# Which free slot a load takes, and when it may take the last one: a decode attention kernel with one slab of 31 slots

## The chip, the cores and the metric

The kernel runs on one core of a Trainium2 chip. The metric is the time of one execution on the device, in microseconds (us). Times of the profile are counted from the start of its span, which is the first instruction of the profiled execution.

## What is computed

Two layer kinds alternate, each is applied twice, and both passes of attention read the same caches.

```python
Bn, D = 8, 448                  # one new token for each of 8 sequences
Hq, Hkv, Sk, Dh = 16, 8, 4096, 256
def A(x):                       # attention over cached K and V, no mask
    q = x @ wq                  # (8, 16, 1, 256)
    p = softmax(q @ k_cache.T / 16)      # each K head serves two q heads
    return (p @ v_cache) @ wo
def B(x):                       # h shifted along a sequence of length 1, so the first
    ...                         # w1/w2 part adds nothing; what is left:
    return x + gelu(layernorm(x) @ w3) @ w4
x = x + A(layernorm(x));  x = x + B(layernorm(x))
x = x + A(layernorm(x));  x = x + B(layernorm(x))
```

K and V are 8 sequences x 8 heads x 4096 x 256 in bf16, 134 MB each. They don't fit on the chip, so most of them is read twice, and 447 MB come from HBM in one execution.

## The kernel before

**Units and steps.** A unit is `(pass, sequence b, head g)`: the scores, the softmax and the product with V of one K/V head. Pass 1 is the first attention layer and pass 2 the second. The list `units` holds 128 units and some empty places (`GAP`) in a written-out order: for each sequence b the heads of pass 1, then a layer end where the dense layers of that sequence run (spread over steps by the generator `mid_steps`), then pass 2. To have work for the gap, two heads of other sequences (`loose`, `ahead`, `lone`) are drawn into it. A unit takes four steps, and step number i is 4 x (place of the unit) + quarter. In step i the main loop calls `transposes(i)`, then `k_part` (16 products with one transposed quarter of K), on the first steps of a unit the softmax of the unit before it (`max_mms`, `exps`, `to_rows`, `sums`), then `v_part` for the quarters of V that `plan` puts there, some six steps after their K, and one piece of the dense layers.

**Slots.** All of K and V passes through one SBUF tile, `slab`, cut into 31 slots of 512 KB (128 partitions x 2048 bf16). A slot holds a quarter of a unit's K as loaded (raw), a quarter of its K transposed (`kt`), or a quarter of its V. The list `free` says which slots the program may fill. `transposes` takes a free slot for the transposed quarter, lets VectorE (DVE) transpose into it with two instructions at L562, and puts the raw slot on the list; `v_part` (products at L630) and `k_part` (L653) put their slot on the list once its products are issued. In pass 1 the transposed K of heads 2 to 7 (`KEEP`) isn't given back: it stays in the slab for pass 2 of the same sequence, apart from two quarters that are parked in PSUM (copied back by ScalarE at L520).

**Loads.** The order of all loads is fixed beforehand in `loads`. `pump`, called after every slot that comes free, issues from that list on the SP queue (L536) as long as more than `RESERVE` = 1 slot is free, so one slot is always left for the next transposition. A load is a quarter (512 KB, a single) or two neighbouring quarters into slots x and x + 1 with x even (1 MB, a pair), where the list allows it (`wide`). Where it is also in `firm`, and at least seven quarters are under way, the load waits for two neighbouring slots rather than go out as a single. SP runs its queue in order: a load whose slot is still being read holds up all loads behind it.

`take` gives the lowest number among the free slots whose neighbour isn't free, or else the lowest of all; `take_two` gives the lowest free even pair. The list `free` itself is in the order in which the program gave the slots back.

**Who waits.** DVE does the transpositions and, in the same queue, the two maxima (L668, L686) and the sum (L727) of the softmax; PE needs the first maximum for its products at L676. Two transpositions of a quarter are due in step i for K that is used in step i + 1 (`LEAD`) and beyond; `by[i]` says how many quarters must be transposed by then, evenly over a stretch between layer ends, so most are transposed 5 to 18 steps ahead of use. `transposes` returns early where the next quarter isn't yet due and either its load hasn't been issued or no slot is free.

Of the kernel before, what the change touches and what calls it, by code (L numbers as in the profile page):

```python
# [15 lines left out]
UNIT = 2048  # L16
N_SLOTS = 31
RESERVE = 1
KEEP = 6
PARKED = 2  # L20
RUN = 2
# [10 lines left out]
def kernel(  # L32
# [164 lines left out]
    def flush():  # L197
        while between:
            between.pop(0)()
# [162 lines left out]

    heads = list(range(G))
    loose = heads[: G - KEEP]

# [5 lines left out]
    lone = {b: [(1, b + 2, g) for g in loose] for b in range(4)}  # L373
# [24 lines left out]
    def fresh(u, s):  # L398

        return u is not GAP and (u[0] == 1 or u[2] in loose)  # L400
# [4 lines left out]
    t = 0  # L405
# [21 lines left out]
    parts = [(t, s) for t in range(n_units) for s in range(4) if fresh(units[t], s)]  # L427
# [16 lines left out]
    for t in order:  # L444
        for s in range(4):
            i = late_v.get((t, s), 4 * t + s + LAG)
            if t in ends or units[t + 1 : t + 2] == [GAP]:
                i = 4 * t + (6, 6, 7, 7)[s]
            elif t + 2 == n_units:
                i = 4 * t + (7, 8, 8, 8)[s]  # L450
            elif t + 1 == n_units:
                i = 4 * t + (5, 5, 6, 6)[s]
# [3 lines left out]
    loads = []  # L456
# [5 lines left out]
    for i in range(4 * n_units + 8):  # L462
# [9 lines left out]
        t, q = divmod(i + 2, 4)  # L472
# [3 lines left out]
    free = list(range(N_SLOTS))  # L476
# [3 lines left out]
    def take():  # L480

        lone = [x for x in free if x ^ 1 not in free]
        x = min(lone or free)
        free.remove(x)
        return x

    def take_two():

        both = [x for x in free if x % 2 == 0 and x + 1 in free]
        if both:  # L490
            free.remove(both[0])
            free.remove(both[0] + 1)
        return both[:1]
# [13 lines left out]
    extra.append((w4_sb[:], B_w4.rearrange("(c p) d -> p c d", p=128)))  # L507
    n_loads = [0]

    def pump():  # L510
        while loads and len(free) > RESERVE:
            kind, t, i = loads[-1]
            _, b, g = units[t]
            if kind == "p":
                loads.pop()
                x = take()
                dst = slots[x].rearrange("p (e q c x) -> p q c e x", e=4, q=2, c=4)
                for j in range(2):
                    src = park[parked[g, i]][j][:].bitcast(BF16)
                    nc.scalar.copy(dst[:, j], src.rearrange("p (c e x) -> p c e x", c=4, e=4))  # L520
                kt_of[(1, b, g), i] = x
                continue
            cache, of = (A_k_cache, raw_of) if kind == "k" else (A_v_cache, v_of)
            n, two = 1, (kind, t, i + 1)
            if i % 2 == 0 and two in wide and two in loads[-PAIR_VIEW:]:
                x = take_two() if len(free) > RESERVE + 1 else []
                if x:
                    n, x = 2, x[0]
                    loads.remove(two)
                elif under_way[0] >= ENOUGH and two in firm:  # L530
                    return
            loads.pop()
            if n == 1:
                x = take()
            src = cache[b, g].rearrange("(p s e) d -> p s (e d)", s=4, e=8)
            nc.sync.dma_start(  # L536
                slab[:, UNIT * x : UNIT * (x + n)].rearrange("p (s d) -> p s d", s=n),
                src[:, i : i + n],
            )
            for m in range(n):  # L540
                of[t, i + m] = x + m
            under_way[0] += n
            n_loads[0] += n
            if n_loads[0] >= 8 and extra:
                nc.sync.dma_start(*extra.pop(0))

    todo = list(reversed(parts))

    def transposes(i):


        while len(parts) - len(todo) < by[i]:
            t, s = todo[-1]
            if 4 * t + s > i and ((t, s) not in raw_of or not free):
                return
            todo.pop()
            raw = raw_of.pop((t, s))
            kt = kt_of[units[t], s] = take()
            src = slots[raw].bitcast(FP32).rearrange("p (q c e i) -> p q c e i", q=2, c=4, e=4)
            dst = slots[kt].bitcast(FP32).rearrange("p (e q c r) -> p q c e r", e=4, q=2, c=4)  # L560
            for q in range(2):
                nc.vector.transpose(dst[:, q], src[:, q])  # L562
            _, b, g = units[t]
            if (g, s) in parked:
                for q in range(2):
                    dst = park[parked[g, s]][q][:].rearrange("p (c e r) -> p c e r", c=4, e=4)
                    nc.vector.transpose(dst, src[:, q])
            free.append(raw)
            under_way[0] -= 1
            pump()  # L570
# [5 lines left out]
    def dense_next():  # L576
        flush()
        if dense and next(dense[0], "end") == "end":
            dense.pop(0)
# [3 lines left out]
    def make_blocks(t):  # L583

        if t in runs and t not in ready:
            p, b, g = units[t]
            if p == 1 or (b, g % 4 // 2) in q_done:
                x, n = runs[t]
                qT = qT1[:, :, b] if p == 1 else qT2[:, :, b % 2]
                expand(Qblk[x], qT[:, 4 * g : 4 * (g + n)], n, scb[t % 2])  # L590
                ready.add(t)
# [50 lines left out]
    def k_part(t, s):  # L642
        u = units[t]
        p, b, g = u
        if s == 0:
            assert t not in runs or t in ready
            scs[t] = scb[t % 2][:, 0:64].rearrange("p (c b h) -> p c b h", b=4, h=2)
        key = (u if fresh(u, s) else (1, b, g)), s
        ktv = slots[kt_of[key]].rearrange("p (e c m x) -> p e c m x", e=4, c=2, x=2)
        for c in range(2):  # L650
            for db in range(4):
                for x in range(2):
                    nc.tensor.matmul(  # L653
                        scs[t][:, 2 * s + c, :, :],
                        ktv[:, db, c, :, x],
                        Qblk[run_of[t][0]][:, run_of[t][1], db, x, :, :],
                        start=(db == 0 and x == 0),
                        stop=(db == 3 and x == 1),
                    )
        if p == 2 or g in loose or (g, s) in parked:  # L660
            free.append(kt_of.pop(key))
            pump()
# [9 lines left out]
    def max_mms(t):  # L672

        mzs[t] = scb[t % 2][:, 64:384]
        for h in range(2):
            nc.tensor.matmul(  # L676
                mzs[t][:, 128 * h : 128 * h + 128],
                pm[:, h : h + 1].to_broadcast([128, 128]),
                ident,
                start=True,  # L680
                stop=True,
            )
# [42 lines left out]
    def sums(t):  # L725
        zz = mzs[t][:, 256:320].rearrange("p (c h) -> p h c", h=2)
        nc.vector.tensor_reduce(zs, zz, AX.X, ALU.add)  # L727
        rz_of[t] = rzs[nth[t] % 2]
        if (t, 0) in late_v:
            rz_of[t] = rz_far[:, held.index(t) % AHEAD, :]  # L730
        nc.gpsimd.tensor_tensor(out=rz_of[t], in0=zs, in1=mone, op=ALU.pow)  # L731
# [60 lines left out]
    for t in range(n_units + 1):  # L792
        cur = t < n_units
        for q in range(4):
            i = 4 * t + q
            if cur:
                if t in fence and q == 0:
                    flush()
                    while (fence[t], 1) not in q_done:
                        next(dense[0])  # L800
                        flush()
                    flush()
                    make_blocks(t)
                late = q == 0 and t and not beside[t]
                if beside[t]:
                    transposes(i)
                flush()
                if not late and not beside[t]:
                    transposes(i)
                if units[t]:  # L810
                    k_part(t, q)
            back = t and units[t - 1]
            if q == 0 and back:
                max_mms(t - 1)
                exps(t - 1)
            if cur and late:
                transposes(i)
            if back and q == 1:
                to_rows(t - 1)
                sums(t - 1)  # L820
            if q == 1 and not cur:
                mark(t - 2)
            for u, s in plan.get(i, []):
                v_part(u, s)
                if s == 3:
                    head_out(u)
            if q == 3 and cur and t > 1 and t - 2 not in ends:
                mark(t - 2)
            if q == 3 and t - 1 in ends:
                mark(t - 1)  # L830
            dense_next()
            if q > 1:
                make_blocks(t + 1)
            if cur and units[t] and q == 3:
                max_reduce(t)
# [112 lines left out]
```

## Time and profile before

| | |
|---|---|
| median of 3 runs | 1114.25 us (1113.67 to 1115.25) |
| profiled execution, its own time | 1115.99 us |
| its span | 1114.2 us |
| granted TensorE clock | 1.0 |
| busy: PE, DVE, ACT, POOL | 62%, 49%, 27%, 9% |
| read from HBM | 446.77 MB |
| loads of V: 1 MB, 512 KB | 130, 252 |
| loads of K: 1 MB, 512 KB | 97, 126 |
| median time from issue to landing, V: 1 MB, 512 KB | 13.1 us, 8.1 us |
| median time from issue to landing, K: 1 MB, 512 KB | 14.0 us, 8.8 us |

In the page's second part the span is cut into 40 slices; a digit is the busy share in tenths, and the last row is what the DMA engines moved. A row of an answer about waits reads: engine, line and what it wrote, what it waited for, us in total, times, longest. A row of windows reads: the window, its length, then for each engine its busy us and number of instructions, then the granted clock, the DMA engines' mean share and GB/s. A row of the timeline reads: start, us, engine, line, operation, written <- read, number of instructions merged into the row, and in brackets the idle time of the engine before it with what ended it. Consecutive instructions of one kind are merged into one row.

### The profile page before, as it was taken

The page shows a single profiled execution, that of the slowest core. Times are in us where ns is not written, and L with a number is a line of the kernel's source. Part 1 is how long each engine was busy: PE and PEld are TensorE (multiplying, and loading weights), DVE is VectorE, ACT ScalarE, POOL GpSimd, SP SyncE. Part 2 cuts the span into 40 slices and gives each one's busy share as a digit, 9 for nine tenths or more (in the row PEclk, how much of TensorE's full clock was granted, in tenths as well). Part 3 has the DMA queues.
Part 4 walks back from the last instruction along what each step waited for, and adds up shares of the span by engine and source line. Part 5 has one row for each costly group of instructions (what it writes and reads, how often), then busy time and mean ns, then how long its engine had stood idle before and what let it go on. Part 6 is the DMA issues. An engine that isn't in the chain of part 4 may idle for free.

```text
span 1114.2 us, 46349 instructions
## 1 busy us (share of the span) xinstructions
PE 687.9 (62%) x20737; PEld 640.8 (58%) x20737; DVE 550.7 (49%) x1305; ACT 306.0 (27%) x1360; POOL 104.1 (9%) x156
## 2 busy tenths in 40 slices
PE   3345675666756576565756667565756667665766
PEld 2334565565646565565655556565656566555765
DVE  4347554654446445554455535563446535554322
ACT  1112124321233212422243212422143212422242
POOL 0001001110011100110011000110011000100011
DMA  9999999999999999999999999999999999999993
GB/s 367 394 418 425 408 417 422 424 417 395 417 423 424 400 403 419 423 424 391 414 420 424 402 410 404 420 424 415 383 421 424 409 412 404 422 423 400 371 405 128
DMA packets 94503, 449.77 MB, mean 404 GB/s; under 512 B 9936, under 2 KB 15968, under 8 KB 64864
## 3 DMA queue, kind: packets, MB, share of 16 engines
q1 hardware_dynamic: 94304, 446.81, 98.4%
q8 instruction: 162, 2.65, 0.9%
q14 instruction: 37, 0.30, 0.1%
HBM read 446.77 MB, written 0.01 MB: 401 GB/s over the span
## 4 chain that ended last, share of the span: by engine, by line
DMA 39%; PE 15%; issue 6%; ACT 6%; DVE 5%; POOL 0%; SPq 0%; DVEq 0%; ACTq 0%; POOLq 0%
DMA slab<-in_A_v_cache_dram 31%; DMA slab<-in_A_k_cache_dram 9%; PE bank L630 5%; PE bank L653 4%; DVE slab L562 3%; ACT pt L720 2%; PE bank L137 1%; ACT slab L520 1%; ACT pe L689 1%; DVE small L686 1%; PE bank L676 1%; PE bank L712 1%; ACT pt_far L720 1%; PE bank L702 1%; PE bank L313 1%
## 5 line engine op out<-in xcount | busy, mean ns | idle before, releaser
L562 DVE STREAM_TRANSPOSE slab<-slab 128x512 f32<-128x512 f32 x640 | 414.6, 687 | 214.7 <-DMA slab<-in_A_k_cache_dram 167.2
L630 PEld LDWEIGHTS <-slab 128*128 128x128 bf16 x8192 | 273.1, 106 | 286.5 <-DMA slab<-in_A_v_cache_dram 223.0
L630 PE MATMUL bank<-pt,slab 128*128 128x2 bf16 x7168 | 260.5, 166 | 232.7 <-DMA slab<-in_A_v_cache_dram 161.5
L653 PE MATMUL bank<-Qblk,slab 128*128 128x8 bf16 x8192 | 297.2, 168 | 77.4 <-DVE slab L562 39.1
L653 PEld LDWEIGHTS <-slab 128*128 128x128 bf16 x8192 | 267.8, 105 | 88.2 <-DVE slab L562 46.6
L689 ACT ACTIVATE pe<-bank,small 128x32 bf16<-128x32 f32 x256 | 61.3, 295 | 406.7 <-DVE small L686 406.7
L731 POOL TENSOR_TENSOR small<-small 128x2 f32<-128x2 f32 x112 | 78.2, 698 | 773.2 <-DVE small L727 773.2
L720 ACT CAST pt<-bank 32x64 bf16<-32x64 f32 x448 | 90.8, 203 | 106.4 <-PE bank L712 102.5
L686 DVE TENSOR_REDUCE small<-bank 128x2 f32<-128x256 f32 x128 | 54.1, 423 | 103.2 <-PE bank L676 102.9
L727 DVE TENSOR_REDUCE small<-bank 128x2 f32<-128x64 f32 x128 | 27.1, 212 | 118.5 <-ACT pt L720 102.9
L166 ACT CAST Qblk<-bank 32x32 bf16<-32x32 f32 (+1 forms) x272 | 48.2, 177 | 110.7 <-PE bank L160 108.2
L676 PE MATMUL bank<-rows,small 128*128 128x128 bf16 x256 | 48.5, 293 | 11.5 <-DVE small L668 11.5
L668 DVE TENSOR_REDUCE small<-bank 128x2 bf16<-128x64 f32 x128 | 26.4, 206 | 58.5 <-PE bank L653 58.3
L630 PE MATMUL bank<-pt_far,slab 128*128 128x2 bf16 x1024 | 37.0, 166 | 26.1 <-DMA slab<-in_A_v_cache_dram 24.4
L712 PE MATMUL bank<-pe,rows 128*128 128x64 bf16 x512 | 51.3, 241 | 1.9 <-issue 1.9
L712 PEld LDWEIGHTS <-rows 128*128 128x128 bf16 x512 | 33.8, 124 | 28.4 <-issue 28.1
L702 PE MATMUL bank<-pe,small 128*128 128x64 bf16 x128 | 27.3, 213 | 30.7 <-ACT pe L689 29.4
L182 PEld LDWEIGHTS <-wo_sb 128*128 128x128 bf16 x1152 | 35.5, 104 | 8.8 <-issue 7.7
L182 PE MATMUL bank<-OT,wo_sb 128*128 128x1 bf16 x1024 | 33.2, 165 | 5.6 <-ACT OT L599 4.5
L137 PEld LDWEIGHTS <-wq_sb 128*128 128x128 bf16 x864 | 30.6, 106 | 10.3 <-issue 5.9
L520 ACT COPY slab<-park 128x1024 bf16<-128x1024 bf16 x32 | 30.1, 1029 | 9.4 <-DVE slab L562 9.3
L599 ACT ACTIVATE OT<-bank,small 128x2 bf16<-128x2 f32 x122 | 25.4, 261 | 24.1 <-PE bank L630 22.7
(113 smaller groups left out, 386.5 us busy)
## 6 DMA issues: line engine op xcount, KB each, us to landing
slab<-in_A_v_cache_dram SPq DMA_DIRECT2D x130, 1024.0 KB, 13.1
slab<-in_A_v_cache_dram SPq DMA_DIRECT2D x252, 512.0 KB, 8.1
slab<-in_A_k_cache_dram SPq DMA_DIRECT2D x97, 1024.0 KB, 14.0
slab<-in_A_k_cache_dram SPq DMA_DIRECT2D x126, 512.0 KB, 8.8
wo_sb<-in_A_wo_dram SPq DMA_DIRECT2D x4, 896.0 KB, 11.7
wq_sb<-in_A_wq_dram SPq DMA_DIRECT2D x3, 1024.0 KB, 6.8
w_sb<-in_B_w_dram SPq DMA_DIRECT2D x1, 1568.0 KB, 12.5
w_sb<-in_B_w_dram SPq DMA_DIRECT2D x3, 448.0 KB, 16.7
```

What stands on the lines that cost most here:

```text
L137: nc.tensor.matmul(pv[:, i, j, :], cols(big[:, c, :], m + i * half), rows[:, c, :], start=(i == 0 and j == 0 and c == 0), stop=True, skip_ ...
L166: nc.scalar.copy(dst, src)
L182: nc.tensor.matmul(y[:, c, :], chunk(wo_sb[:, k, :], c), o[:, k, :], start=False, stop=True, skip_group_check=True,)
L562: nc.vector.transpose(dst[:, q], src[:, q])
L630: nc.tensor.matmul(pos[t][:, k, :], vv[:, c, 128 * k : 128 * k + 128], pts[t][:, 8 * s + c, :], start=(t == 0 and s == 0 and c == 0 and k ...
L653: nc.tensor.matmul(scs[t][:, 2 * s + c, :, :], ktv[:, db, c, :, x], Qblk[run_of[t][0]][:, run_of[t][1], db, x, :, :], start=(db == 0 and x ...
L676: nc.tensor.matmul(mzs[t][:, 128 * h : 128 * h + 128], pm[:, h : h + 1].to_broadcast([128, 128]), ident, start=True, stop=True,)
L686: nc.vector.tensor_reduce(nm, mx, AX.X, ALU.max, negate=True)
L689: nc.scalar.activation(pe[:].rearrange("p c b h -> p h (c b)")[:, h], scs[t].rearrange("p c b h -> p h (c b)")[:, h], ACT.Exp, bias=nm[:, ...
L712: nc.tensor.matmul(pp[:, c], sel, pe[:], start=True, stop=True)
L720: nc.scalar.copy(pts[t][sl].rearrange("p (k c) h -> p k c h", c=4), pp[sl, :, :, pb, :].rearrange("p c k h -> p k c h"),)
L731: nc.gpsimd.tensor_tensor(out=rz_of[t], in0=zs, in1=mone, op=ALU.pow)
```

## The change

Three things change in the schedule that is made when the program is built; no operation is added or taken out.

- `take` gives the slot that has been on the list longest, again first among those whose neighbour isn't free; `take_two` gives the pair whose younger half has been free longest.
- `spare()` takes the place of `RESERVE`: one slot is kept only where the next K to be transposed is used within `SOON` = 4 steps of the current step (`now`), else none.
- `todo`, the K quarters still to be transposed, is made before `pump`, which now reads it.

```diff
+SOON = 4
...
+    now = [0]
...
     def take():
 
         lone = [x for x in free if x ^ 1 not in free]
-        x = min(lone or free)
+        x = (lone or free)[0]
         free.remove(x)
         return x
 
     def take_two():
 
         both = [x for x in free if x % 2 == 0 and x + 1 in free]
+        both.sort(key=lambda x: max(free.index(x), free.index(x + 1)))
         if both:
...
+    todo = list(reversed(parts))
+
+    def spare():
+
+        return RESERVE if todo and 4 * todo[-1][0] + todo[-1][1] <= now[0] + SOON else 0
+
     def pump():
-        while loads and len(free) > RESERVE:
+        while loads and len(free) > spare():
...
             if i % 2 == 0 and two in wide and two in loads[-PAIR_VIEW:]:
-                x = take_two() if len(free) > RESERVE + 1 else []
+                x = take_two() if len(free) > spare() + 1 else []
...
-    todo = list(reversed(parts))
...
-            i = 4 * t + q
+            i = now[0] = 4 * t + q
```

## The prediction

> **What bounds the kernel now.** I read the page first, then windows, then the waits of the SP queue, then the timeline.
>
> ```profile
> DMA  9999999999999999999999999999999999999993
> GB/s 367 394 418 425 408 417 422 424 417 395 417 423 424 400 403 419 423 424 391 414 420 424 402 410 404 420 424 415 383 421 424 409 412 404 422 423 400 371 405 128
> HBM read 446.77 MB, written 0.01 MB: 401 GB/s over the span
> DMA 39%; PE 15%; issue 6%; ACT 6%; DVE 5%; POOL 0%; SPq 0%; DVEq 0%; ACTq 0%; POOLq 0%
> ```
>
> The DMA engines are the bound: busy in every slice but the last, while PE is busy 62% and DVE 49% of the span. Nothing removes bytes here, so time can only come from slices that move less than the best. Windows of 14 us show how much less (last two columns: DMA share, GB/s):
>
> ```profile
> 250.00:264.00 14.00, 8.15 (x234) 7.60 (x230) 4.53 (x15) 2.87 (x15) 0.70 (x1) 1.00 1.00 375
> 280.00:294.00 14.00, 9.86 (x321) 9.59 (x318) 6.50 (x13) 3.91 (x19) 1.25 (x2) 1.00 1.03 416
> 336.00:350.00 14.00, 9.54 (x299) 8.94 (x299) 9.80 (x21) 4.43 (x22) 2.09 (x3) 1.00 1.01 423
> 1036.00:1050.00 14.00, 11.23 (x359) 10.92 (x358) 4.68 (x17) 3.41 (x16) 1.24 (x2) 1.00 0.97 364
> 1050.00:1064.00 14.00, 9.57 (x295) 9.13 (x293) 4.75 (x12) 7.34 (x23) 1.40 (x2) 1.00 0.97 349
> ```
>
> Pairs (1 MB) move 423 to 425, a full run of singles (512 KB) 416. Around each layer end it falls to 350 to 400. Cutting the span into windows of 14 us and summing 14 x (1 - rate/416) over those below 416, start and tail apart, gives 18 us lost, all near the layer ends, and 1036:1064 alone 4.0. That is the most this change can win. Why it falls there:
>
> ```profile
> SPq L536 <- PE bank L630: 202.2, 174, 5.0
> SPq L536 <- DMA slab<-in_A_v_cache_dram: 138.1, 120, 5.2
> SPq L536 <- DVE slab L562: 97.6, 49, 6.0
> SPq L536 <- PE bank L653: 81.2, 64, 8.3
> ```
>
> Loads wait on SP for the release of their slot: by a V quarter's products (L630), a transposition (L562) or a K quarter's products (L653). At a layer end six heads' transposed K lie in the slab, some nine slots circulate, and each load goes out within 0.1 us of the release of a slot just freed. Adding up the trace's issues less its packets, in steps of 2 us, with the shortfall beside it: with 1 to 1.5 MiB issued and not yet moved, 8.4% of the rate is lost (62 us of the span); with 1.5 to 2, 4.1% (168 us); with 2 to 2.5, 1.5% (198 us); with 2.5 to 3, 0.4%; above, under 1%. So the price of a slot less in the air is known.
>
> **Part 1: oldest slot instead of lowest number.** No instruction is added; 832 quarters of 512 KB are loaded as before. I followed the slot lists of both programs and gave each load, as its earliest moment, the time at which the trace of before shows the last release of its slot. Example, the first dip: the third K quarter of unit 29 waits in before for a transposition
>
> ```profile
> 250.57 0.33 SPq L536 DMA_DIRECT2D slab<-in_A_k_cache_dram  x1
> 249.24 1.30 DVE L562 STREAM_TRANSPOSE slab<-slab 128x512 f32<-128x512 f32 x2
> 258.38 1.30 DVE L562 STREAM_TRANSPOSE slab<-slab 128x512 f32<-128x512 f32 x2 [4.08 <-DMA slab<-in_A_k_cache_dram]
> ```
>
> (SP's load starts as the first two transpositions end, 250.5). In the new order it takes a slot released at 249.2, 1.4 us sooner; and it is this quarter's landing for which DVE idles 4.08 us before 258.38. Of the 21 loads from 252.4 to 277.8, 12 gain 0.4 to 3.4 us, seven wait for the same release as before (six of them transpositions: 259.7, 265.9, 268.6 and so on), and two lose under 0.8. In the stretches that lose, the mean lead is 0.15 to 0.45 MiB; I take 0.25.
>
> That is half a bin above, so each bin goes half way to the next: 62 x (8.4-4.1)%/2 = 1.3, 168 x (4.1-1.5)%/2 = 2.2, 198 x (1.5-0.4)%/2 = 1.1, together 4.6 us. Against it: what moves sooner is no longer outstanding, so lead is spent as it is used; for it: K landing sooner frees the next slots sooner. Bounds 0 and 8 (half of the loss); I take **-3.6 us**, nearer the worked value since the example feeds on.
>
> DVE's own waits for a target slot (L562 waiting for L630: 40.4 us) and ACT's copies from the parked banks also take older slots. The copy at L520 waited 3.94 us for a transposition and held PE 6.6 us (315.7 to 322.3), yet the rate there stayed at 425: at nothing, since 4.4 MiB outstanding cover it; uncovered it would be those 6.6.
>
> **Part 2: the last slot.** Where the next K is over four steps off, loads go down to no free slot (198 loads are issued so). Mostly this is where eight transfers are already outstanding and SP waits for the eighth-last to land (the DMA row of the waits, 138 us; the load at 296.2 goes out as the one eight before it lands at 296.1): no gain, counted in the lead above. Its price is on DVE. With no free slot, `transposes` returns; in each of seven layers six transpositions that stood between steps 56 and 64 (128 to 136, and so on) come all at once at step 65 (137, ...), 12 instructions in a row:
>
> ```profile
> 297.69 0.43 DVE L686 TENSOR_REDUCE small<-bank 128x2 f32<-128x256 f32 x1 [0.86 <-PE bank L676]
> 298.03 1.29 DVE L562 STREAM_TRANSPOSE slab<-slab 128x512 f32<-128x512 f32 x2
> 300.14 0.22 DVE L727 TENSOR_REDUCE small<-bank 128x2 f32<-128x64 f32 x1 [0.81 <-ACT pt L720]
> 302.72 0.23 DVE L668 TENSOR_REDUCE small<-bank 128x2 bf16<-128x64 f32 x1 [1.14 <-PE bank L653]
> ```
>
> Six at 1.30 take 298.1 to 305.9, L727 and the next two transpositions end at 307.4, and L668, behind them in DVE's queue, runs 4.7 us late. PE waits for it at L676, so the products of step 140 and the releases behind them too. The next load, at 303.6 in before, then goes out at 310.1. Cover: at 302.7 there are 3.65 MiB outstanding, at 0.40 MiB/us until 311.9. So it just holds; and later the 6.6 us of the parked copy are no longer lost, so the lag is made up by 320. At the other places the burst begins with 2.4 to 3.1 MiB outstanding, and two or three loads that don't hang on step 140 still go out. Bounds 0 and 4.7 each; I take 0.07 each, near covered, **+0.5 us**.
>
> **Part 3: pairs.** Singles fall from 378 to 366, pairs rise from 227 to 233. Two singles at 416 take 2.52 us, a pair at 424 2.47: 6 x 0.05 = **-0.3 us**. By the median times to landing (two times 8.1, against 13.1) it would be 6 x 3.1 = 18.6 if nothing overlapped; eight in flight overlap, so I take the rates. The Trainium skill, "DMA: Bandwidth & Descriptors", "Anatomy of one DMA", gives each transfer a fixed 2.0 us besides its bytes (a fit for another issuing path); by it, six transfers fewer would be 12 us, an estimate. The window of singles at 416 speaks against it.
>
> **Part 4: the end.** From step 551 loads wait for two neighbouring slots. Oldest-first scatters the free slots: four to ten are free where before had one to six, and the last ten loads have releases 0 to 6.2 us later (the very last at 1083.5, not 1081.1). Before had 2.4 to 4.6 MiB outstanding from 1058 to 1070, so this reaches a lossy level only near 1058 to 1062 and 1070: about 6 us at some 8% more, **+0.5 us**. Bounds 0 and 6.2. Data still lands last near 1096, and the 18 us of tail behind it stay.
>
> Sum: -3.6 + 0.5 - 0.3 + 0.5 = **-2.9 us**. The profiled execution took 1115.99 (span 1114.2, 1.8 around it), the runs' median is 1114.25, 1.7 less; so 1113.1 profiled and **1111.3 us** as median. A measurement of this kernel tells about 0.2%, 2.2 us.
>
> **Rivals.**
> - The lead is spent at the gates. A third of the loads of a dip wait for the same transposition in both orders, and SP is in order. Then part 1 gives 0.5 to 1: 1113.5 us (1112.1 to 1115). For: equal releases at 259.7, 265.9, 268.6. Against: those transpositions wait for K quarters that are issued sooner. 0.18.
> - The dips mostly close. Then 6 to 10 us: 1106.5. For: DVE's 4.08 us wait is for a quarter now issued 1.4 us sooner, and releases feed on each other. Against: at 1036:1064, the largest dip, leads of up to 4 us turn to lags after 1057. 0.15.
> - Slower: the DVE burst. Its place is step 65 of each layer, PE at L676. It decides where less than 7.4 us x 0.40 = 3.0 MiB is outstanding behind the last load that goes out before step 140 (302.7 to 310.1 above). With 1.2 us exposed in each of seven layers: +8.4 - 3.4 = 1119 us (1116.5 to 1122). For: L668 has no way past twelve instructions, and the third to seventh places start lower than the second. Against: the 3.65 MiB above, and the DVE time that is free before the burst. 0.17.
> - Fewer, larger transfers pay their whole time to landing (the 18.6 us above): 1096 us. 0.02.
> That the change does nothing is excluded: the order of issues and pairs differs.
>
> **Numbers.** The forecast's own case (1108.9 to 1112.8) has 0.48, of which 0.40 lies beyond 2.2 us. Faster 0.40 + 0.15 + 0.02 = 0.57; same 0.08 + 0.18 = 0.26; slower 0.17. The range 1106 to 1117 leaves out the lower end of the second rival (0.04), the last rival (0.02) and most of the third (0.13).
>
> **What would show it.** Right: windows at the layer ends (250:264, 378:392, 518:532, 630:644) at 385 to 400 instead of 370; a run of 12 transpositions before a late maximum (L668 now) in each of seven layers, with the rate there still at 416 or more; the 6.6 us stand of PE before the parked copies gone; 233 pairs. Wrong: rates at the layer ends unchanged, or a new dip below 400 some 10 us after each burst, or below 400 between 1064 and 1090.

## The result, and the profile after

The changed kernel takes 1120.41 us (median of 6 runs, 1118.37 to 1123.31) against 1114.20 (6 runs, 1113.67 to 1115.69) of the kernel before on the same chip: ratio 1.0053, 95% interval 1.0040 to 1.0066. By this ratio it is 5.9 us slower (the medians differ by 6.2); the forecast was 2.9 faster. The profiled execution took 1119.69 us with a span of 1117.8, 3.6 longer than before's. Before's profile was taken from an execution 1.8 above its median, this one from an execution 0.7 below, so the two profiles show 3.6 of some 6 us. In the changed kernel the load is L545, 9 lines further down, and what stands behind it is 7 further down (transposition L569, products with V L637 and with K L660, maxima L675 and L693, sum L734).

The page of the changed kernel (rate by slices, bytes, chain of waits by engine):

```profile
GB/s 368 395 419 425 409 416 413 424 414 407 416 410 423 414 393 419 424 424 386 416 420 424 423 393 418 380 424 419 408 379 424 422 416 385 417 423 405 377 409 112
HBM read 446.77 MB, written 0.01 MB: 400 GB/s over the span
DMA 60%; PE 17%; DVE 7%; issue 7%; ACT 6%; SPq 2%; POOL 1%; DVEq 0%; ACTq 0%; POOLq 0%
```

The bytes are the same, and DMA is the bound still. Slices that were low are higher (the tenth 395 to 407, the twenty-third 402 to 423), and slices that were good are low: the twenty-sixth falls from 420 to 380, the thirtieth from 421 to 379. Windows of 14 us of the changed kernel (last column GB/s):

```profile
250.00:264.00 14.00, 8.13 (x238) 7.60 (x235) 5.34 (x16) 2.85 (x14) 0.70 (x1) 1.00 1.01 403
378.00:392.00 14.00, 7.55 (x224) 7.08 (x221) 4.76 (x10) 3.66 (x18) 1.40 (x2) 1.00 1.02 406
518.00:532.00 14.00, 9.30 (x265) 8.77 (x264) 5.37 (x16) 2.79 (x14) 0.70 (x1) 1.00 0.99 373
700.00:714.00 14.00, 10.06 (x311) 9.30 (x309) 7.64 (x16) 8.44 (x28) 1.40 (x2) 1.00 0.92 351
812.00:826.00 14.00, 7.56 (x226) 6.96 (x226) 11.56 (x22) 3.43 (x16) 0.91 (x2) 1.00 0.90 359
1036.00:1050.00 14.00, 11.10 (x355) 10.73 (x353) 3.98 (x21) 3.35 (x16) 1.94 (x3) 1.00 1.01 405
1050.00:1064.00 14.00, 10.21 (x319) 9.69 (x316) 6.45 (x14) 5.22 (x21) 1.41 (x2) 1.00 0.93 341
```

Of the four layer ends that the prediction named, three rose as forecast: 250:264 from 375 to 403, 378:392 from 370 to 406, 630:644 from 371 to 421. The fourth, 518:532, rose only from 368 to 373, and 658:672 fell from 417 to 374. At the end, 1036:1050 rose from 364 to 405. But 700:714 and 812:826 stand at 351 and 359, where before has 420 and 419, with a DVE that is busy for 11.56 us at 812. The timeline of DVE in the changed kernel, at the second and the fifth of the seven places of the burst:

```profile
298.50 8.00 DVE L569 STREAM_TRANSPOSE slab<-slab 128x512 f32<-128x512 f32 x12 [0.52 <-PE bank L637]
...
307.76 0.19 DVE L675 TENSOR_REDUCE small<-bank 128x2 bf16<-128x64 f32 x1
...
689.61 8.00 DVE L569 STREAM_TRANSPOSE slab<-slab 128x512 f32<-128x512 f32 x12 [0.37 <-PE bank L637]
...
698.87 0.19 DVE L675 TENSOR_REDUCE small<-bank 128x2 bf16<-128x64 f32 x1
```

The twelve transpositions are there as foretold, and the maximum behind them runs at 307.8, 5.0 us later than before (forecast 4.7). What the prediction had not seen is who stands first in line. These are SP's queue beside the fifth burst, and SP's waits in 690:705 and in 812:830:

```profile
691.20 0.33 SPq L545 DMA_DIRECT2D slab<-in_A_v_cache_dram  x1
699.01 0.33 SPq L545 DMA_DIRECT2D slab<-in_A_k_cache_dram  x1
```

```profile
SPq L545 <- DVE slab L569: 11.5, 2, 7.4
SPq L545 <- DVE slab L569: 10.5, 3, 8.2
```

One load waits 7.4 us for a transposition that stands behind the burst, and in order behind it wait all other loads. Outstanding bytes (issues less packets) fall from 2.9 MiB at 690 to 0.8 at 698 and 0.6 at 702, and the four steps of 2 us from 698 to 706 lose 24, 33, 22 and 64% of 420 GB/s. At the second place the next load goes out at 310.1 as forecast; outstanding bytes fall to 0.7 MiB until then, and the step behind it loses 29%.

The seven places differ. The load that waits for a transposition behind the burst stands for 6.8, 5.9, 4.7, 4.7, 7.4, 8.2 and 7.4 us. The fewest bytes outstanding behind the burst are 0.7, 0.7, 1.8, 1.8, 0.1, 0.0 and 0.3 MiB, and the windows there lose 0.5, 0.7, 0, 0, 2.2, 2.4 and 1.2 us. When the burst begins, 2.7 MiB are outstanding at the first two places and 3.1 to 3.3 at the last three, which lose most. So the places are told apart by how long SP stands, not by what is outstanding when the burst begins.

Over the span, SP's waits for transpositions rise from 97.6 to 176.5 us and the longest from 6.0 to 8.2. The rise of the sum needs no burst: e3 below, which has none, has 179.0. Two of SP's rows for the whole span:

```profile
SPq L545 <- PE bank L637: 187.6, 164, 4.5
SPq L545 <- DVE slab L569: 176.5, 80, 8.2
```

The quarter of the prediction's example goes out at 249.97, not 1.4 but 0.6 us sooner than before, and DVE waits for it a little longer (4.59 us, before 4.08). SP's row first, then DVE's:

```profile
249.97 0.38 SPq L545 DMA_DIRECT2D slab<-in_A_k_cache_dram  x1
258.62 1.30 DVE L569 STREAM_TRANSPOSE slab<-slab 128x512 f32<-128x512 f32 x2 [4.59 <-DMA slab<-in_A_k_cache_dram]
```

**Where the 3.6 us are.** As in the prediction I sum 14 x (1 - rate/416) over windows below 416, on one grid from 42 to 1078, in three groups: the ten windows of the bursts (168, 308, 434, 448, 574, 700, 812, 826, 938 and 952), the end (1036 to 1078), and the rest, which is the layer ends. On this grid before has 0.0, 4.0 and 15.0 us, the changed kernel 7.1, 3.4 and 10.4. So the layer ends give 4.6 and the end 0.6, and the bursts take 7.1: +1.9. The last data lands 3.4 us later (1099.2, not 1095.8). Of the 1.5 between, 1.0 is in windows that move 416 or more, which this sum counts as full, and the rest lies outside the grid. The tail behind the last data grew by 0.2.

### The profile page after: what moved, and what is told of

It reads as the page before. It is cut to its first block, busy times and chain, and to the rows that moved or that the text cites. A ratio compares the mean times of both kernels' runs of the same rounds, so it can differ in the third digit from the quotient of the medians.

```text
span 1117.8 us, 46323 instructions
## 1 busy us (share of the span) xinstructions
PE 688.7 (62%) x20737; PEld 643.5 (58%) x20737; DVE 551.2 (49%) x1305; ACT 306.3 (27%) x1360; POOL 104.4 (9%) x156
## 4 chain that ended last, share of the span: by engine, by line
DMA 60%; PE 17%; DVE 7%; issue 7%; ACT 6%; SPq 2%; POOL 1%; DVEq 0%; ACTq 0%; POOLq 0%
DMA slab<-in_A_v_cache_dram 43%; DMA slab<-in_A_k_cache_dram 16%; PE bank L637 6%; DVE slab L569 5%; PE bank L660 5%; ACT pt L727 2%; PE bank L138 2%; ACT slab L529 1%; SPq L545 1%; PE bank L683 1%; PE bank L719 1%; ACT pe L696 1%; DVE small L693 1%; DMA wq_tl<-in_A_wq_dram 1%; PE bank L709 1%
## 5 line engine op out<-in xcount | busy, mean ns | idle before, releaser
L569 DVE STREAM_TRANSPOSE slab<-slab 128x512 f32<-128x512 f32 x640 | 413.8, 687 | 166.1 <-DMA slab<-in_A_k_cache_dram 159.1
L637 PEld LDWEIGHTS <-slab 128*128 128x128 bf16 x8192 | 275.4, 106 | 257.1 <-DMA slab<-in_A_v_cache_dram 209.1
L637 PE MATMUL bank<-pt,slab 128*128 128x2 bf16 x7168 | 260.6, 166 | 207.5 <-DMA slab<-in_A_v_cache_dram 147.2
L660 PE MATMUL bank<-Qblk,slab 128*128 128x8 bf16 x8192 | 297.0, 168 | 98.6 <-DVE slab L569 39.0
L660 PEld LDWEIGHTS <-slab 128*128 128x128 bf16 x8192 | 268.7, 105 | 109.1 <-issue 61.1
L693 DVE TENSOR_REDUCE small<-bank 128x2 f32<-128x256 f32 x128 | 54.4, 425 | 110.9 <-PE bank L683 110.6
L675 DVE TENSOR_REDUCE small<-bank 128x2 bf16<-128x64 f32 x128 | 26.8, 209 | 122.6 <-PE bank L660 120.1
L734 DVE TENSOR_REDUCE small<-bank 128x2 f32<-128x64 f32 x128 | 26.8, 209 | 99.7 <-ACT pt L727 89.1
L683 PE MATMUL bank<-rows,small 128*128 128x128 bf16 x256 | 48.7, 294 | 21.7 <-DVE small L675 19.7
L637 PE MATMUL bank<-pt_far,slab 128*128 128x2 bf16 x1024 | 37.2, 166 | 24.8 <-DMA slab<-in_A_v_cache_dram 22.7
L138 PEld LDWEIGHTS <-wq_sb 128*128 128x128 bf16 x864 | 30.5, 106 | 11.1 <-issue 6.6
L138 PE MATMUL bank<-small,wq_sb 128*128 128x1 bf16 x768 | 27.9, 165 | 6.1 <-issue 6.1
```

The lines of the kernel that those rows point to most:

```text
L138: nc.tensor.matmul(pv[:, i, j, :], cols(big[:, c, :], m + i * half), rows[:, c, :], start=(i == 0 and j == 0 and c == 0), stop=True, skip_ ...
L637: nc.tensor.matmul(pos[t][:, k, :], vv[:, c, 128 * k : 128 * k + 128], pts[t][:, 8 * s + c, :], start=(t == 0 and s == 0 and c == 0 and k ...
L660: nc.tensor.matmul(scs[t][:, 2 * s + c, :, :], ktv[:, db, c, :, x], Qblk[run_of[t][0]][:, run_of[t][1], db, x, :, :], start=(db == 0 and x ...
L683: nc.tensor.matmul(mzs[t][:, 128 * h : 128 * h + 128], pm[:, h : h + 1].to_broadcast([128, 128]), ident, start=True, stop=True,)
L693: nc.vector.tensor_reduce(nm, mx, AX.X, ALU.max, negate=True)
```

## The experiments

Three thoughts were to be told apart: the burst on DVE is what costs; the oldest slot costs by itself; the last slot does, by the transpositions that it delays. The kernels ran on several chips, on which the median of before was 1114.2 to 1115.7 us, so the ratio to before on the same chip is what compares; where an expectation gives a time, it takes before at 1114.3 if it names no other. "+us" is the ratio's excess x 1114.2, with its interval. The next columns are from the one profiled execution: the sum of lost time in the three groups of windows, the landing of the last data, and the start of the last softmax sum.

| kernel | pairs | +us (95%) | bursts, layer ends, end | last data | last sum |
|---|---|---|---|---|---|
| before | 227 | | 0.0, 15.0, 4.0 | 1095.8 | 1099.6 |
| after | 233 | 5.9 (4.5 to 7.4) | 7.1, 10.4, 3.4 | 1099.2 | 1103.3 |
| e1_spread | 235 | 4.5 (3.0 to 5.9) | 3.0, 12.0, 4.4 | 1097.0 | 1100.7 |
| e2_burst | 226 | 7.6 (6.2 to 8.9) | 8.8, 12.8, 4.2 | 1103.9 | 1107.8 |
| e3_oldest | 227 | 3.0 (1.9 to 4.1) | 0.6, 15.2, 4.5 | 1097.3 | 1102.4 |
| e4_last | 225 | 5.1 (3.8 to 6.5) | 11.1, 7.6, 3.3 | 1100.8 | 1105.8 |
| e5_wanted_oldest | 225 | 4.2 (2.9 to 5.7) | 1.1, 17.3, 4.2 | 1100.3 | 1104.4 |
| e6_wanted_lowest | 231 | 4.1 (2.5 to 5.7) | 0.9, 15.1, 2.7 | 1096.0 | 1099.9 |
| e7_oldest_no_wait | 215 | 2.7 (1.6 to 3.9) | 0.1, 15.0, 2.1 | 1095.2 | 1100.1 |
| e8_oldest_at_dips | 231 | 4.9 (3.3 to 6.5) | 0.8, 15.9, 3.3 | 1097.0 | 1101.6 |
| e9_highest | 228 | 3.0 (2.0 to 4.0) | 0.1, 17.1, 2.1 | 1096.4 | 1102.2 |
| e10_oldest_to_480 | 226 | 2.6 (1.6 to 3.6) | 1.0, 16.2, 1.5 | 1096.1 | 1101.2 |
| e11_oldest_from_480 | 230 | 1.0 (0.0 to 1.9) | 0.2, 13.2, 4.2 | 1095.5 | 1100.1 |
| e12_half_burst | 223 | 0.9 (-0.7 to 2.3) | 0.0, 15.2, 1.8 | 1094.8 | 1100.0 |
| e13_last_rarely | 222 | 2.8 (1.7 to 4.0) | 0.2, 15.3, 3.4 | 1098.2 | 1102.3 |
| e14_last_spread_lowest | 231 | 2.0 (0.8 to 3.1) | 1.5, 14.6, 2.5 | 1095.8 | 1100.5 |

The runs of one kernel scatter by 1 to 8 us, and a profile is one of them. The profiles of e1, e6 and e8 are their fastest runs, those of e4, e5 and e13 their slowest, that of e2 its second slowest. The windows are fixed in time, while a layer end moves by some us from kernel to kernel, so a loss near the edge of a window can change groups: e14, which has no burst, has 404 at 798:812 and 376 at 812:826, where before has 377 and 419. The windows tell roughly where time goes, the ratio how much.

### The burst

**e1_spread**: the changed kernel without its bursts.

```diff
     def transposes(i):
+        n = 0
         while len(parts) - len(todo) < by[i]:
             t, s = todo[-1]
+            n += 1
+            if n > 1 and 4 * t + s > i + LEAD:
+                return
```

> The changed kernel with one edit: in a step, at most one quarter is transposed ahead of its due step (more only where it is used in the next step), so the six transpositions that pile up at step 65, 137, ... come one per step. Slots, the last-slot rule and pairs otherwise as changed (235 pairs). Theory A (the burst of twelve transpositions makes PE and then SP late, and the DMA engines run dry behind it: about 9 us of new dips in the profile after, at 168, 308, 700, 812 to 840 and 938 to 966): the dips go, the gains at the layer ends stay, so 1111 us (1107 to 1114), faster than before. Theory B (the price is the scatter: oldest-first takes and waits for two neighbouring slots): the dips and the time stay as changed, 1118 to 1122 us. Theory C (the price is the last slot itself: without a free slot K is transposed late): some dips stay, 1115 to 1119.

+4.5 us. The windows of the bursts fall from 7.1 to 3.0, but the layer ends come back from 10.4 to 12.0, and the medians differ by less than the intervals. Theory A's 1111 us didn't come: without its bursts the changed kernel is still slower than before, so the burst isn't all of it. In e1, 97 transpositions run later than in before, which may cost too.

**e2_burst**: the kernel before, with six transpositions held back at the seven places (the new line stands behind the early return of `transposes`).

```diff
+HOLD = (72, 144, 216, 288, 356, 424, 492)
...
+            if any(u <= 4 * t + s < u + 6 and i < u - 7 for u in HOLD):
+                return
```

> The kernel before with one edit: the same six transpositions in each of seven layers are held back to step 65, 137, ... and come in a row; lowest-number slots and one slot kept, as before (226 pairs). Theory A: the burst alone makes new dips behind it; each costs 0.7 to 2.8 us in the profile after, so +5 to +10 us: 1119 to 1124. Theory B: no change by the burst, 1113 to 1115. Theory C: the burst costs little where a slot is kept, 1114 to 1117.

+7.6 us: the burst alone makes the kernel slower, by more than the whole change. Windows of before, and one of e2_burst:

```profile
378.00:392.00 14.00, 8.15 (x246) 7.70 (x244) 4.96 (x11) 4.07 (x20) 1.39 (x2) 1.00 0.99 370
518.00:532.00 14.00, 9.03 (x265) 8.52 (x263) 5.09 (x17) 2.48 (x13) 0.89 (x2) 1.00 1.00 368
700.00:714.00 14.00, 7.57 (x233) 7.03 (x231) 4.46 (x10) 6.95 (x20) 0.70 (x1) 1.00 1.02 420
```

```profile
700.00:714.00 14.00, 8.28 (x256) 7.69 (x253) 7.21 (x15) 7.79 (x24) 1.40 (x2) 1.00 0.85 311
```

At 700:714 the rate falls from 420 to 311. The edit has one side effect: loads behind a held-back transposition take other slots than before (226 pairs), and what that costs isn't told apart here. 8.8 us are lost in the burst's windows, and the layer ends gain 2.2.

**e12_half_burst**: the same with `u + 3 <=` in place of `u <=`. Three are held back, DVE runs three in a row twice, and no run is longer.

> The kernel before with three transpositions of each of seven layers held back, in place of six, so that DVE runs three in a row twice at each place and no run is longer (3 x 1.30 = 3.9 us of lag at a time, in place of 7.8). Theory of cover (a lag costs only what goes beyond the bytes outstanding, 2.4 MiB or more at 0.40 MiB/us, thus 6 us): 1114 to 1115.5 us. Theory of proportion (every us that the products are late is lost, whatever is outstanding): half of the 7.4 us of six in a row, thus 1117.5 to 1119 us.

+0.9, with an interval that holds zero; nothing is lost in the burst's windows:

```profile
700.00:714.00 14.00, 7.32 (x227) 6.75 (x228) 6.17 (x15) 6.63 (x18) 0.94 (x2) 1.00 1.02 421
```

Outstanding bytes don't fall below 1.3 MiB there (690 to 708; 0.1 in e2_burst), and SP's longest wait is 3.3 us (8.0 in e2_burst). That fits the theory of cover and not that of proportion: half the lag costs little or nothing, and half of 7.6 lies outside the interval. Where between three and six the price begins wasn't measured.

### The order of the slots

**e3_oldest**: the changed kernel with `return RESERVE` in `spare`, so only the oldest-first order is left.

> Part 1 alone: oldest slot first in both takes, one slot always kept (227 pairs, no held-back transposition, no burst). Theory A: only the gains at the layer ends, less what the scatter at the end costs: 1110 us (1106 to 1113). Theory B: the scatter makes it slower than before, 1116 to 1121. My prediction's part 1 gave -3.6 and part 4 +0.5: 1111.

+3.0 us, and no gain at the layer ends: 15.2 us lost against 15.0. Windows of e3_oldest and its SP waits:

```profile
378.00:392.00 14.00, 8.15 (x240) 7.69 (x241) 4.72 (x10) 3.84 (x20) 1.40 (x2) 1.00 0.97 366
518.00:532.00 14.00, 8.89 (x254) 8.54 (x255) 4.32 (x15) 3.27 (x16) 0.70 (x1) 1.00 1.00 363
...
1050.00:1064.00 14.00, 9.27 (x287) 8.89 (x288) 5.25 (x12) 4.01 (x19) 1.41 (x2) 1.00 0.90 330
```

```profile
SPq L545 <- DVE slab L569: 179.0, 88, 6.6
```

366 and 363, where before has 370 and 368. Over the span, loads wait for transpositions 88 times in place of 49, 179 us in place of 97.6: more often than before, the slot that was longest on the list is one whose transposition is still to run. The end is worse as well, 330 in place of 349, and there the sum of the last unit comes 2.8 us later (DVE's last sum, before and then e3_oldest):

```profile
1099.59 0.22 DVE L727 TENSOR_REDUCE small<-bank 128x2 f32<-128x64 f32 x1 [2.11 <-ACT pt L720]
```

```profile
1102.39 0.23 DVE L734 TENSOR_REDUCE small<-bank 128x2 f32<-128x64 f32 x1 [2.12 <-ACT pt L727]
```

**e7_oldest_no_wait**: e3_oldest, and a load at the end goes out as a single rather than wait for two neighbours.

```diff
-                elif under_way[0] >= ENOUGH and two in firm:
+                elif under_way[0] >= ENOUGH and two in firm and t < 136:
```

> e3_oldest with one edit: in the last units (from place 136 on) loads no longer wait for two neighbouring slots; 215 pairs instead of 227, and one slot free instead of four to ten. Theory B (oldest-first scatters the free slots, and loads that wait for neighbours come late): a good part of the 3.7 us of e3 comes back, 1115 to 1117, and the dip of 1.1 us at 1064 to 1078 goes. If the scatter costs elsewhere or not at all: 1118 to 1120.

+2.7 in place of +3.0. The end's loss falls from 4.5 to 2.1 us and the last data comes 2.1 sooner, but the median hardly moves. So the scatter of slots at the end isn't most of what the oldest slot costs.

**e10_oldest_to_480 and e11_oldest_from_480**: e3_oldest with the oldest-first order (in both takes) in one part of the steps, the lowest number in the other.

```diff
-        x = (lone or free)[0]
+        x = (lone or free)[0] if now[0] < 480 else min(lone or free)
```

> Oldest free slot in both takes up to step 480, lowest number from there on; one slot always kept. Theory A: the loss lies in the seven layers, 1116.5 to 1118.5 us. Theory B: the end is what oldest costs, so 1114 to 1115.5 us with a tail under 18.6 us. Had the oldest slot the gain at the layer ends that the prediction gave it, and only the end against it, then 1111 to 1112.

> The other half: lowest number up to step 480, oldest from there on; one slot always kept. Theory A: one layer in eight, 1114.5 to 1115.5 us. Theory B: 1116.5 to 1118.5 us, with the sum of the last unit late and a tail of 19.4 us or more, as with oldest throughout.

+2.6 and +1.0. The sum, 3.6, is e3's 3.0 within the intervals. Most of the cost comes with the layers up to step 480, as the theory of order has it (with before at 1115.7 here, its 1116.5 to 1118.5 and 1114.5 to 1115.5 read +2.2 to 4.2 and +0.2 to 1.2). The tail of 19.4 or more that the other theory gave to e11 alone is in e10 (19.7, last sum at 1101.2), and e11 has 19.3.

**e9_highest**: the control. The kernel before with `max` in place of `min` in `take`.

> The kernel before with `take` giving the highest number (max) in place of the lowest; nothing else. A control: a third order, with no claim to be better at anything. Theory A (the slot order sets which reader each load waits for, and any order other than the one the rest was fitted to loses some 3 us somewhere): 1117 to 1119 us, with new windows below 410 GB/s at places where before has none. Theory B (the oldest slot costs 3 to 4 us for a reason of its own, the scatter of free slots at the end and the later last data and tail): 1114 to 1115.5 us, tail behind the last data at 18.4 us.

+3.0: an order that nobody chose for a purpose costs what the oldest-first order does. So a cost of the oldest slot's own isn't needed to explain e3, though one such order can't exclude it. One place is easily read, the load of the same K quarter (the 41st that is loaded) on SP's queue (e9_highest, then before):

```profile
110.37 0.43 SPq L536 DMA_DIRECT2D slab<-in_A_k_cache_dram  x1
```

```profile
103.75 0.43 SPq L536 DMA_DIRECT2D slab<-in_A_k_cache_dram  x1
```

In 98:112, SP waits three times for a transposition (8.9 us in all) where before waits once (5.3). This load goes out 6.6 us later than in before, the pair of K quarters ahead of it 11.7 us later (106.86, not 95.18), and the windows 98:112 and 112:126 move 393 and 374 GB/s, not 427 and 411. From the 40th of the 512 quarters of K on, the first product of each comes later than in before, by 0.7 to 6.9 us. Over the whole span, though, e9 waits no longer for transpositions than before (93.8 us, before 97.6), but longer for products with V (236.9, before 202.2). So what its loads wait for isn't what those of e3 wait for.

### The last slot

**e4_last**: the changed kernel with the lowest number, so only the last slot is left (`x = min(lone or free)`, and no sort in `take_two`).

> Part 2 alone: the last slot given out where no K is due within four steps, lowest number first as before (225 pairs; bursts of six at step 65, 137, ...). Theory A: the burst's price without the gains of the oldest slot: 1120 to 1126 us. Theory B: 1113 to 1116. Theory C: as A, 1118 to 1124.

+5.1. It has the burst, 11.1 us lost there, and the best layer ends of all, 7.6.

**e14_last_spread_lowest**: e4_last with e1's three lines in `transposes`, so no burst.

> Lowest number as in before, last slot as in the changed kernel (196 loads), and at most one transposition per step ahead of LEAD, so no run of six: the run of two is the commonest. Against e4_last (the same with runs of six, +5.1 us): theory A (the burst is what the last slot costs) +0 to 1.5 us over before; theory of order (the oldest slot is what was left in e1) the same; theory of delays (the 96 transpositions that still run one to nine steps late cost by themselves) +3 to 4.5, as e1 and e6.

+2.0, below what the theory of delays gave (3 to 4.5) and just above the other's 1.5; the interval reaches into both. With the burst, the gain at the layer ends goes too (14.6, before 15.0): in these profiles the two come together. e4 less e14 gives the burst a price of 3.1 us beside the last slot, e1 less e14 the oldest slot one of 2.5, each with an interval of about 2 us to both sides.

**e5_wanted_oldest and e6_wanted_lowest**: one slot is kept also where a transposition is already due; e5 takes the oldest slot, e6 the lowest.

```diff
     def spare():
+        wanted = len(parts) - len(todo) < by[max(now[0], 0)]
-        return RESERVE if todo and 4 * todo[-1][0] + todo[-1][1] <= now[0] + SOON else 0
+        return RESERVE if todo and (wanted or 4 * todo[-1][0] + todo[-1][1] <= now[0] + SOON) else 0
```

> The changed kernel with one edit: the last slot is also kept where the planned pace already wants a further quarter transposed (the count is behind by[i]). 283 quarters are then transposed in the step of before and 37 one step later, so no burst; 225 pairs; 171 loads still take the last slot. Theory A (bursts cost 7 us, the oldest slot costs about 3 by its scatter, the last slot gains 5 or more at the layer ends): 1112 us (1109 to 1115). Theory B (the scatter carries most of the loss): 1117 to 1121. Theory C (any late transposition costs, one step too): 1117 to 1121 as well, but then e6 is slow too.

> As e5_wanted_oldest, but with the lowest number in take as before (231 pairs): the last slot alone, without bursts and without scatter. Theory A: 1109 us (1106 to 1113), faster than before. Theory B: 1110 to 1114. Theory C: 1117 to 1121.

+4.2 and +4.1, where theory A gave times below before's. Theory C's 1117 to 1121 us came. Neither has a burst, 37 transpositions run one step late, and neither gains at the layer ends (17.3 and 15.1).

**e8_oldest_at_dips**: e5 with the lowest number outside the layer ends.

```diff
-        x = (lone or free)[0]
+        x = min(lone or free) if calm[min(now[0] // 4, n_units)] else (lone or free)[0]
```

> As e5_wanted_oldest, but the oldest slot is taken only outside the calm stretches, where loads are singles; in the calm stretches, where pairs are formed, take gives the lowest number as before (231 pairs). Theory A and B: no scatter where pairs are made, so it's at or below e6: 1107 to 1112. If the oldest slot also costs among singles: above e6 by 1 to 4 us.

+4.9, not the 1107 to 1112 us of theories A and B. No gain at the layer ends either (15.9). Its distance to e6 (+4.1) is within the intervals.

**e13_last_rarely**: e4_last with `SOON = 20`. 49 loads take the last slot, and two transpositions run late.

> Lowest number as in before, and the last free slot only where the next K is over 20 steps off: 49 loads take it (198 in the changed kernel) and two transpositions run later than in before, by one and four steps (97 in e1, 37 in e5). If the last slot costs by the transpositions that it delays: within 0.15% of before (1114 to 1117 us where before is 1115.7). If taking the last slot costs by itself, in proportion to the loads that do: a quarter of some 4 us, +1. If it helps where it delays nothing: 1 us or more below before.

+2.8, although it delays next to nothing. So delayed transpositions aren't needed to lose 2 to 3 us, and the loss isn't in proportion to the loads that take the last slot. What e13 shares with e3, e9 and e10 is that slots fall to other loads than before.

## Why the prediction was wrong

Two terms failed, and each was measured alone. The order of the slots (parts 1 and 4) was forecast at -3.1 us, and e3 has +3.0; the last slot (part 2) was forecast at +0.5, and e4 has +5.1. Added up they would give +8.1; together in the changed kernel they give +5.9. The range ended 3.4 us below the measured median. The third rival (slower by the DVE burst, 0.17 of the chances) came nearest: its price of +8.4 at the bursts stands against 7.1 in the windows of the changed kernel, and its +4.8 in all (1119) against +5.9. That the total came so near is in part luck, since the rival kept -3.4 for the other three parts, and e1, the changed kernel without bursts, is still 4.5 slower than before.

**Part 2, the last slot, was mis-sized.** The twelve transpositions, their length (8.0 us, forecast 7.8), the lateness of the maximum and the next load at 310.1 were right. The step that failed is the price of 0.07 us a place, "near covered". The windows of the changed kernel lose 0 to 2.4 us a place, 1.0 on average, and the burst alone (e2) costs 7.6 / 7 = 1.1. The cover was read from before's trace, 3.65 MiB at 302.7; in the changed kernel 2.6 MiB are outstanding at that moment. And the queue that waits first was named wrongly: not only PE's products behind the late maximum, but SP, of which one load waits 4.7 to 8.2 us for a transposition behind the burst. That loads go out that don't hang on step 140 doesn't help where SP stands still. The three places that lose most had the most bytes outstanding as the burst began, so the other number that the prediction gave, 2.4 to 3.1 MiB, didn't tell them apart. The reasoning itself, bytes outstanding against lag, fits e12: a lag of 3.9 us was covered, one of 7.8 not. The stand of PE before the parked copies shrank from 6.6 to 4.2 us; it wasn't gone.

The Trainium skill, "TensorE: Matmul & The Clock Gate", "Architectural detail: the array is 16× 32×32, not 1× 128×128", says that the queue of VectorE is strictly first in, first out. The trace agrees: L675, whose products PE needs, runs at 698.87, directly behind twelve transpositions, the sum and two more transpositions.

**Part 1, the oldest slot, had the wrong sign.** The -3.6 us were forecast at the layer ends. The changed kernel does gain 4.6 there, which looks like a success; but e3, the oldest slot alone, gains nothing there (15.2 against 15.0) and loses 3.0 in all. The prediction's own count, seven of 21 loads that "wait for the same release as before", six of them for transpositions, was a warning, and the first rival (lead spent at the gates) describes what this part does at the layer ends, though its +0.5 to 1 us of gain isn't there. The gain that the changed kernel shows comes with the last slot and the burst: e4 has 7.6, e2 12.8, while e14 without the burst has 14.6. The step that failed was to take leads from a list with the releases of before's trace. Of the 21 loads of the example, 12 were to gain 0.4 to 3.4 us. In the changed kernel the 21 go out 0.1 us sooner on average and none by more than 1.0; in e3 they go out 0.4 later on average, and one alone is sooner (0.9). The example itself went out at 249.97, not at 249.2. The likely reason, argued and not shown, is that each load that goes out sooner or later moves the releases that follow it. The table of loss against bytes outstanding, by which the lead was priced, isn't what failed: counted anew it gives 4.0 us in place of 4.6.

**Part 3**: 233 pairs came as forecast, and count for as little. The Trainium skill, "DMA: Bandwidth & Descriptors", "Anatomy of one DMA", has 2.0 us fixed for a transfer on another issuing path; e7 with 215 pairs has 12 transfers more than e3, an estimate of +24 by it. Measured are +2.7 in place of e3's +3.0, so such a price doesn't add up here, where several transfers are outstanding at once.

**Part 4, the end.** 1050:1064 fell from 349 to 341, and the group of the end didn't lose (3.4, before 4.0), against +0.5 forecast; in e3 it lost the 0.5 (4.5). "Data still lands last near 1096" was wrong for the changed kernel, 1099.2.

**What stays open.** Each order of slots that isn't before's cost 1 to 3 us: oldest, highest, oldest in one part, or 49 loads in the last slot. e9 shows at one place how a later load lowers the rate; that it is so at the others is argued, not shown, and e3 and e9 lose by different waits. How much of the 7.6 us of e2 is the burst and how much the other slots that its loads take is open as well. Why no order tried was better than before's was not settled, and no kernel here beats before.

## What to carry to other kernels

A queue that is served in order makes the choice of a buffer a choice of whom to wait for: price a new order of buffers by replaying it with the releases that it makes itself, and run an order without any purpose beside it, which tells what another order may cost by itself. Instructions in a row on an engine that others wait for cost little here where the bytes outstanding outlasted the wait that they caused (three transpositions in a row), and much where they didn't (six). Read that wait and that cover in the kernel that has the burst, place by place. A gain in the windows one had aimed at is no proof of its cause until the part alone shows it.

## What the runs showed of the hardware and had not been expected

The end of the span follows the last softmax sum, not the last data. In all 16 profiles the span ends 14.5 to 14.7 us after the start of that sum, while the time from the last data to the end varies from 18.4 to 20.5 (e9_highest: data 0.6 us later than before, sum 2.6 later, span 2.7 longer). e12 landed its data 1.0 us before the kernel before and ended 0.4 after it.

The loss against bytes outstanding is steep at the low end, of which before's trace has only some 10 us. Below 1 MiB the changed kernel and e2_burst lose a quarter to a third of the rate, by how a packet in flight is counted; from 1 to 1.5 MiB it is 8 to 13%, from 1.5 to 2 MiB 4 to 6%.
